# Where the norm products of the next batch stand, and the order of the opening, in an attention and soft-MoE kernel

## The chip, the cores and the metric

One core of a Trainium2 chip runs the whole program. The time is the device time of one execution in microseconds (us), and the median over executions is compared. The profile describes one execution. Its engines are PE (TensorE, matrix products), PEld (its weight loads), DVE (VectorE), ACT (ScalarE), POOL (GpSimd) and SP, whose queue issues every DMA of this kernel.

## The reference, cut to what matters

```python
# 8 batches, 2496 rows, d_qk = 64, d_model = 256
scores = (1 / S) * z @ z.T             # symmetric: queries and keys are both z
out = u * (maximum(scores, 0) ** 2 @ v)
x = out.reshape(19968, 256)
logits = x @ phi                       # 32 slots
slot_input = softmax(logits, axis=0).T @ x
slot_out = relu(slot_input @ w1) @ w2  # 8 experts of 4 slots each
result = softmax(logits, axis=1) @ slot_out
```

The attention is nearly all of the work: for each batch a 2496 x 2496 matrix of scores, its squared positive part, and the product of that with v.

## The kernel before, in words

**Steps.** A batch has five chunks of queries (512 columns, the last one 448) and five blocks of keys (512 rows each). A chunk meets a block in two halves of 256 keys. A chunk therefore has ten halves, a batch fifty (the last batch sixty), and the main loop (L942 to L971) takes one half per step; h counts the steps over all batches, and "place" below means h modulo 50. In a step two things happen. `prepare` (L404) makes ready a half that is needed later: h + 2 in the first 19 steps and h + 3 afterwards. `sums_halves` or `sums_whole` adds the half of this step into `acc`, the product with v.

**Prepare.** If the half is computed, PE multiplies z with z into the PSUM tile `sc`, of which there is one. ACT takes the positive part (`r<-sc`) and squares it (`r<-r`). ACT or DVE casts to fp16 (`ph<-r`), and DVE subtracts to get the rest (`pl<-r,ph`). Because the scores are symmetric, a half that another chunk will need is transposed by DVE (`y<-r`, or `yd<-r` for a part of a diagonal block) and stored in DRAM by a DMA (`turned<-y`). A half that is there already ("turned") is fetched (`r<-turned`), and only the cast and the subtraction are left. At its end `prepare` runs the list `behind`: small work that other parts of the program have put there.

**Sums.** v is held as a high and a low fp16 part, so each half takes twelve products of 512 columns: high and low v with `ph`, high v with `pl`. If the half to be prepared is computed, the sums are cut into two phases of six products, and the product for `sc` and whatever `behind` has for PE stand between the phases.

**The shared bank.** The PSUM pool `ms_ps` holds one tile, and a new tile in it must wait until the last reader of the old one is done. Four users take turns: the norm products (`n<-sq`), the product of `scale_v` (`mx`), the logits of the MoE (`lg<-xg,phi_sb`) and the slot sums (`lg<-xt`, issued together with the logits of the next group of tokens).

**Norms.** z and v of the next batch have to be scaled before they are split into fp16 parts. `load_z` (L124) loads a block of z and gives three actions: `squares` (ACT, tile `sq`, one buffer), `norms` (two products with a matrix of ones into the `ms` tile, a maximum by DVE into `few`, and four small DVE instructions that make the factors `norm2` and `z_by`), and `split` (one ACT and one DVE instruction). The table `splits` (L857 to L868) has the five blocks of batch b loaded at places 19 to 23 of the batch before, squared at 21 to 25, their norms taken at 22 to 26, one step after the squares, and split at 29, 31, 33, 39 and 41. v follows: loads at places 25 to 34, its squares at 27 to 36, `largest` (three small DVE instructions) at 38, `scale_v` (L204: a small product `mx`, a DVE maximum and small DVE instructions) at 40, the splits at 42 to 51.

**Logits.** When two chunks of 512 tokens are complete, `groups` (L251) makes a list of 15 small pieces of MoE work, of which the loop pops one per step at steps with `x.at > 1` (L948). The first piece is the logits with the slot sums of the group before. They fall where the count of pieces puts them: place 22 and 42 for the steps in which the z blocks of batches 1, 2, 4 and 6 are measured, and place 2, 12 and 32 for batches 3, 5 and 7.

**Opening.** L919 to L940: DVE sets a constant, SP issues the loads, PE runs products on a constant (`keep_busy`, tile `idle`) to stay occupied, and for each of the five blocks of z in turn come squares, norms, and the scaling of z in place. After blocks 0 and 1 halves 0 and 1 are prepared. Then come the ten squares of v, `largest`, `scale_v` and the first split, and the loop begins. The first twelve halves are scored from fp32 z.

Of the kernel before, what the change touches and what calls it, by code (L numbers as in the profile page):

```python
# [8 lines left out]
F32 = mybir.dt.float32  # L9
# [9 lines left out]
P = 128  # L19
# [6 lines left out]
QC = 512  # L26
# [35 lines left out]
def bits(ap):  # L62
    return ap.bitcast(I32)
# [14 lines left out]
def attn_soft_moe_kernel(ctx, tc, uT, v, zz, phi, ww, outT):  # L78
# [29 lines left out]
    def pair(name, n):  # L108
        return [cpool.tile([P, n], F32, name=f"{name}{i}") for i in range(2)]

    norm2, z_by, energy, v_by, out_by, few = (
        pair(name, n)
        for name, n in (("norm2", NP), ("z_by", NP), ("energy", 2 * NP), ("v_by", 2 * NP), ("out_by", NP), ("few", 4))
    )

    def take_blocks(b):


        for j in BLOCKS[b == B - 1]:
            zt[b, j] = blk.tile([P, 2, 512], F16, tag="blk", name=f"z_{b}_{j}")  # L120
        for i in range(2 * NP):
            vt_[b, i] = blk.tile([P, 2, 2, D], F16, tag="blk", name=f"v_{b}_{i}")

    def load_z(b, j):  # L124


# [6 lines left out]
        n2, by = (t[b % 2][:, j : j + 1] for t in (norm2, z_by))  # L133
        square = []

        def squares():
            sq = raws.tile([P, 512], BF16, tag="sq", name=f"sq_{b}_{j}", bufs=1)
            act.activation(sq, raw, AF.Square, bias=nudge)
            square.append(sq)

        def norms():
            ps = ms_ps.tile([P, 2, 512], F32, tag="ms", name=f"n2_{b}_{j}")
            for h, rows in enumerate(HALF):
                pe.matmul(
                    ps[:, h, 0:256], ones[rows, 0:P], square[0][rows, 256 * h : 256 * h + 256],
                    start=True, stop=True,
                )
# [22 lines left out]
        return squares, norms, split  # L170

    def load_v(b, i):
        raw = raws.tile([P, 2, D], F32, tag="raw", name=f"vr_{b}_{i}", bufs=NRAW)
        sp.dma_start(raw, v[b, :, 2 * i : 2 * i + 2, :])
        by = v_by[b % 2][:, i : i + 1]

        def squares():
            sq = raws.tile([P, 512], BF16, tag="sq", name=f"vq_{b}_{i}", bufs=1)
# [25 lines left out]
    def scale_v(b):  # L204


        w = few[b % 2]
        ps = ms_ps.tile([P, 2, 512], F32, tag="ms", name=f"mx_{b}")
        for h, rows in enumerate(HALF):
            pe.matmul(  # L210
                ps[:, h, 0:64], w[rows, 0:1].to_broadcast([64, P]), ident[rows, rows],
                start=True, stop=True,
            )
        dve.tensor_reduce(w[:, 2:4], ps[:, :, 0:64], axis=AX.X, op=ALU.max)
        dve.tensor_max(w[:, 1:2], w[:, 2:3], w[:, 3:4])
        dve.tensor_scalar_max(w[:, 1:2], w[:, 1:2], 2.0**-120)
        dve.tensor_scalar(
            bits(w[:, 2:3]), bits(w[:, 1:2]), EXPONENT, EXPONENT, op0=ALU.bitwise_and, op1=ALU.bitwise_xor
        )
        n2 = norm2[b % 2].unsqueeze(2).to_broadcast([P, NP, 2])  # L220
        dve.tensor_scalar(
            v_by[b % 2].rearrange("p (j i) -> p j i", i=2), n2, w[:, 2:3], 2.0**-51, op0=ALU.mult, op1=ALU.mult
        )
        dve.tensor_scalar(
            out_by[b % 2], norm2[b % 2], w[:, 1:2], 2.0**40 / S**2, op0=ALU.mult, op1=ALU.mult
        )
# [350 lines left out]
                work.extend(groups(q))  # L577
            s += w

    late, adding = [], []  # L580


    xt_last = []
# [18 lines left out]
    def groups(q):  # L602
# [17 lines left out]
        def logits():  # L620


            ps = ms_ps.tile([P, 2, 512], F32, tag="ms", name=f"lg_{q}")
            xj = x.rearrange("p c (j t k) -> p c t j k", j=2, k=P)
            for c in range(2):
                for t in range(4):
                    for h, rows in enumerate(HALF):
                        pe.matmul(
                            ps[t * NS : (t + 1) * NS, h, D : 2 * D], phi_sb[rows, c],
                            xj[rows, c, t], start=(c == 0), stop=(c == 1),  # L630
                        )
            if late:
# [224 lines left out]
    splits, later = {}, {}  # L857
    for b in range(1, B):
        base, order = (b - 1) * 2 * NP * NQ, BLOCKS[b == B - 1]
        z_at = [29, 31, 33, 39, 41]  # L860
        v_at = [47, 42, 43, 44, 45, 46, 48, 49, 50, 51]
        for i, (j, at) in enumerate(zip(order, z_at)):
            splits.setdefault(base + 21 + i, []).append((load_z, b, j, [base + 21 + i, base + 22 + i, base + at]))
        for i, at in enumerate(v_at):
            splits.setdefault(base + 27 + i, []).append(
                (load_v, b, i, [base + 27 + i, base + at, base + at])
            )
        later[base + 38] = lambda b=b: largest(b)  # L868
        later[base + 40] = lambda b=b: scale_v(b)
    landing, fetched = {}, set()  # L870

    def transfers(h):

# [13 lines left out]
        for f, b, i, at in splits.get(h + 2, ()):  # L887
            if (b, 0) not in vt_:
                take_blocks(b)
            for step, g in zip(at, f(b, i), strict=True):  # L890
                landing.setdefault(step, []).append(g)
        if h in later:
# [31 lines left out]
    dve.memset(nudge, 2.0**-40)  # L924
    take_blocks(0)
    open_loads()
    constants()
    keep_busy(8)
    for p, (squares, norms) in enumerate(first_z):
        squares()  # L930
        norms()
        if p < 2:
            prepare(p)
        keep_busy(2)
    for f in first_v:
        f()
        keep_busy(2)
    largest(0)
    scale_v(0)
    split_first_v()  # L940
# [1 line left out]
    for h, x in enumerate(halves):  # L942
# [10 lines left out]
        if ahead and not halves[ahead[0]].turned:  # L953
# [318 lines left out]
```

## Time and profile before

| | |
|---|---|
| median of 3 runs | 1422.95 us (1422.49 to 1427.03) |
| the profiled execution's own time | 1428.09 us |
| span of its instructions | 1426.3 us |
| PE busy | 1294.8 us (91%) |
| DVE busy | 1122.3 us (79%) |
| ACT busy | 964.5 us (68%) |
| DMA engines | 69.3% of the span, 210 GB/s |
| granted clock of PE, mean | 0.96 |

A timeline row reads: start, duration, engine, operation, what is written from what, shape, and in brackets how long the engine had been idle and who released it. "x4" products on 64 rows are two pairs that run side by side, one on each half of the array's rows. A product of 512 columns is listed with 0.38 us because its end is modelled; the next one starts 0.216 us later, and that distance is what it costs. A page line of the form "A <- B: 10, 5, 3" in the view of waits means that A waited for B 10 us in total, 5 times, 3 us the longest.

### The profile page before, as it was taken

Reading aid. Unit: us, or ns where it says so; the run is one execution under the profiler, and the core shown is the slowest. Engines: PE = TensorE matmul, PEld = TensorE weight load, DVE = VectorE, ACT = ScalarE, POOL = GpSimd, SP = SyncE. Lnnn points to the kernel's source line nnn. Section 1 sums busy time; section 2 is a strip of 40 time slices with the busy share of each in tenths; the row PEclk is TensorE's granted clock in tenths of the full one; section 3 lists DMA queues with packets and bytes.
Section 4 is the critical chain, followed back from the end, with each engine's and each line's share of the span. In section 5 each row is a group of like instructions: output and inputs, shape, how many; then the busy total and the mean of one; then the engine's idle time right before and its main releaser. Section 6 shows DMA issues by size and latency. Waiting matters only on the chain.

```text
span 1426.3 us, 28005 instructions
## 1 busy us (share of the span) xinstructions
PE 1294.8 (91%) x11069; PEld 618.9 (43%) x11069; DVE 1122.3 (79%) x1685; ACT 964.5 (68%) x1259; POOL 3.7 (0%) x22
## 2 busy tenths in 40 slices
PE   6997999889997999879998999969999899989984
PEld 2343455334543444334553444424454344434752
DVE  4787899588996899768996789857997888867663
ACT  4876788466965878557885768657686668754453
POOL 0000000000000000000000000000000000000000
PEclk9999999999999999989999999989999999999995
DMA  3468838677578747868378855758478874979949
GB/s 126 120 189 246 248 98 213 217 198 225 131 222 259 216 137 179 259 184 254 92 210 260 262 150 140 246 180 232 125 185 256 269 216 115 271 233 298 341 198 383
DMA packets 136404, 298.91 MB, mean 210 GB/s; under 512 B 17872, under 2 KB 38864, under 8 KB 124240
## 3 DMA queue, kind: packets, MB, share of 16 engines
q1 hardware_dynamic: 136272, 297.11, 69.3%
q8 instruction: 87, 1.43, 0.4%
q14 instruction: 45, 0.37, 0.1%
HBM read 162.04 MB, written 113.77 MB: 193 GB/s over the span
## 4 chain that ended last, share of the span: by engine, by line
PE 66%; ACT 14%; DVE 10%; DMA 5%; issue 4%; SPq 1%; DVEq 0%; ACTq 0%
PE acc L74 52%; ACT r L74 8%; PE sc L74 8%; DVE y L74 3%; ACT ph L74 3%; DVE pl L74 3%; PE lg L74 2%; PE pf L74 1%; SPq L74 1%; DMA turned<-y 1%; DMA w_own<-in_w 1%; DVE few L74 1%; DVE ph L74 1%; ACT v L74 1%; ACT ot L74 1%
## 5 line engine op out<-in xcount | busy, mean ns | idle before, releaser
L74 PE MATMUL acc<-ph,v 64*128 64x512 f16 (+5 forms) x5036 | 950.7, 376 | 3.9 <-ACT v L74 2.0
L74 PEld LDWEIGHTS <-v 64*128 64x128 f16 (+1 forms) x7554 | 477.4, 97 | 540.3 <-issue 66.8
L74 PE MATMUL acc<-pl,v 64*128 64x512 f16 (+5 forms) x2518 | 612.0, 376 | 0.3
L74 DVE TENSOR_TENSOR pl<-r,ph 128x1024 f16<-128x1024 f32 (+1 forms) x410 | 466.6, 1145 | 134.5 <-ACT ph L74 108.5
L74 ACT ACTIVATE r<-sc 128x1024 f32<-128x1024 f32 (+1 forms) x242 | 229.3, 947 | 206.9 <-PE sc L74 205.4
L74 ACT CAST ph<-r 128x1024 f16<-128x1024 f32 (+1 forms) x286 | 289.0, 1020 | 118.6 <-PE acc L74 62.6
L74 ACT ACTIVATE r<-r 128x1024 f32<-128x1024 f32 (+1 forms) x242 | 238.8, 987 | 6.9
L74 DVE STREAM_TRANSPOSE y<-r 128x1024 f32<-128x1024 f32 x160 | 198.1, 1238 | 0.0
L74 PE MATMUL sc<-z,z 64*128 64x512 f16 x912 | 124.7, 377 | 2.8 <-ACT r L74 2.5
L74 DVE CAST ph<-r 128x1024 f16<-128x1024 f32 (+1 forms) x124 | 74.2, 599 | 54.3 <-ACT r L74 54.2
L74 PEld LDWEIGHTS <-z 64*128 64x128 f16 x1380 | 71.5, 95 | 78.1 <-issue 10.3
L74 PE MATMUL n<-sq,const-bfloat16-1.0 64*128 64x256 bf16 x80 | 12.9, 316 | 77.6 <-DVE few L74 51.1
L74 DVE SCALAR_TENSOR_TENSOR xg<-acc,out_by,ut 128x1024 f32<-128x1024 f32 (+7 forms) x57 | 51.8, 932 | 20.3 <-PE acc L74 15.9
L74 ACT ACTIVATE v<-vr,v_by 128x512 f16<-128x512 f32 x80 | 57.3, 717 | 2.4 <-DVE v_by L74 2.4
L74 DVE SCALAR_TENSOR_TENSOR v<-vr,v_by,v 128x512 f16<-128x512 f32 x80 | 58.0, 726 | 0.7 <-ACT v L74 0.7
L74 ACT ACTIVATE vq<-vr 128x512 bf16<-128x512 f32 x80 | 49.9, 624 | 10.4 <-DMA vr<-in_v 8.7
L74 PEld LDWEIGHTS <-const-bfloat16-1.0 64*128 64x128 bf16 x156 | 9.3, 112 | 100.8 <-DVE few L74 60.2
L74 PE MATMUL sc<-z 64*128 64x512 f16 (+1 forms) x468 | 51.2, 324 | 0.0
L74 DVE STREAM_TRANSPOSE y<-xg 128x512 f32<-128x512 f32 x72 | 49.5, 687 | 0.0
L74 DVE TENSOR_TENSOR pl<-rd,ph 128x512 f16<-128x512 f32 x36 | 24.2, 672 | 23.6 <-ACT ph L74 23.6
L74 DVE COPY ot<-pf 128x1024 f32<-128x1024 f32 (+1 forms) x20 | 24.0, 1198 | 20.6 <-PE pf L74 19.8
L74 ACT ACTIVATE sq<-zr,nudge 128x512 bf16<-128x512 f32 x35 | 25.1, 718 | 21.4 <-PE n L74 18.6
(177 smaller groups left out, 620.4 us busy)
## 6 DMA issues: line engine op xcount, KB each, us to landing
turned<-y SPq DMA_DIRECT2D x320, 256.0 KB, 4.5
r<-turned SPq DMA_DIRECT2D x76, 1024.0 KB, 6.3
xt<-y SPq DMA_DIRECT2D x288, 72.0 KB, 3.2
vr<-in_v SPq DMA_DIRECT2D x80, 256.0 KB, 5.3
outT<-ot SPq DMA_DIRECT2D x18, 1024.0 KB, 6.9
ut<-in_uT SPq DMA_DIRECT2D x31, 512.0 KB, 5.9
lent<-yd SPq DMA_DIRECT2D x144, 64.0 KB, 2.0
rd<-lent SPq DMA_DIRECT2D x36, 256.0 KB, 5.3
```

Source lines behind the costliest of these rows:

```text
L74: return lambda *a, **k: self.tc.keep_in_program_order(f(*a, **k))
```

## The change

- **Later norms.** The five blocks of z are loaded at places 9, 11, 13, 15 and 17. A new function, `measure`, runs in every step. It takes a block's norm products only if its squares were issued at least two steps before, if neither norms nor logits have used the bank in this step or the one before, and, up to place 25, only if the half being prepared is computed. It then issues the squares of the next block if fewer than two squared blocks are waiting. `sq` has two buffers, and the squares of v have a tile of their own.
- **Small steps once per batch.** The DVE maximum goes into `tops`; the four small instructions move into `factors`, which runs once for all five blocks. `scale_v` uses one instruction in place of two.
- **Places.** The splits of z move from 29, 31, 33, 39, 41 to 31, 32, 33, 39, 41, and `scale_v` from 40 to 41.
- **Opening.** An ACT instruction on the constant is issued ahead of the first data. The five squares follow one another, and the norm products go to five different PSUM places, so that none waits for another's maximum. z blocks are scaled one by one as they are needed. Halves 0 to 3 are prepared ahead of the loop, with the squares of v between them; steps 0 and 1 of the loop prepare nothing.

```diff
         def squares():
-            sq = raws.tile([P, 512], BF16, tag="sq", name=f"sq_{b}_{j}", bufs=1)
+            sq = raws.tile([P, 512], BF16, tag="sq", name=f"sq_{b}_{j}", bufs=2)
...
-        def norms():
-            ps = ms_ps.tile([P, 2, 512], F32, tag="ms", name=f"n2_{b}_{j}")
+        def norms(ps=None):
+            if ps is None:
+                ps = ms_ps.tile([P, 2, 512], F32, tag="ms", name=f"n2_{b}_{j}")[:, :, 0:256]
...
-            w = few[b % 2][:, 0:2]
-            dve.tensor_reduce(w, ps[:, :, 0:256], axis=AX.X, op=ALU.max)
-            dve.tensor_max(n2, w[:, 0:1], w[:, 1:2])
-            dve.tensor_scalar(bits(n2), bits(n2), EVEN, None, op0=ALU.bitwise_and)
-            dve.tensor_scalar(
-                bits(by), bits(n2), EVEN, 1, op0=ALU.bitwise_xor, op1=ALU.logical_shift_right
-            )
-            dve.tensor_scalar_mul(by, by, 2.0**77)
-            if b == 0:
-                dve.tensor_scalar_mul(raw, raw, by)
+            dve.tensor_reduce(tops[b % 2][:, 2 * j : 2 * j + 2], ps, axis=AX.X, op=ALU.max)
...
+    def factors(b, js=slice(0, NP)):
+        n2, by = (t[b % 2][:, js] for t in (norm2, z_by))
+        t = tops[b % 2].rearrange("p (j h) -> p h j", h=2)[:, :, js]
+        dve.tensor_max(n2, t[:, 0], t[:, 1])
...
-        z_at = [29, 31, 33, 39, 41]
+        z_at = [31, 32, 33, 39, 41]
...
-            splits.setdefault(base + 21 + i, []).append((load_z, b, j, [base + 21 + i, base + 22 + i, base + at]))
+            splits.setdefault(base + 11 + 2 * i, []).append((load_z, b, j, base + at))
...
-        later[base + 40] = lambda b=b: scale_v(b)
+        later[base + 41] = lambda b=b: scale_v(b)
...
+    unmeasured, squared, used = [], [], [-9, 0]
+
+    def measure(h, scoring):
+        n = h % (2 * NP * NQ)
+        if squared and squared[0][0] <= h - 2 and used[0] <= h - 2 and (scoring or n >= 26):
+            behind.append(squared.pop(0)[1])
+            used[0] = h
+            used[1] += 1
+            if used[1] % NP == 0:
+                behind.append(lambda: factors(used[1] // NP))
+        if unmeasured and unmeasured[0][0] <= h and len(squared) < 2:
+            _, squares, norms = unmeasured.pop(0)
+            behind.append(squares)
+            squared.append((h, norms))
...
+    act.activation(few[1][:, 0:1], nudge, AF.Square)
     constants()
+    keep_busy(6)
...
+    for p in range(NP):
+        first_z[p][0]()
+    first_z[0][1](places[0])
+    factors(0, slice(0, 1))
+    raise_z(0)
+    for p in range(1, NP):
+        keep_busy(1)
+        first_z[p][1](places[p])
+    factors(0, slice(1, NP))
+    raise_z(1)
+    for p in range(4):
+        measure_v((2, 2, 1, 1)[p])
+        prepare(p)
+        if p < 3:
+            raise_z(p + 2)
     keep_busy(8)
...
+    measure_v(4)
     largest(0)
     scale_v(0)
     split_first_v()
...
         if work and (x.at > 1 or last <= 20):
+            n = len(bursts)
             work.pop(0)()
+            if len(bursts) > n:
+                used[0] = h
         behind.extend(landing.pop(h, ()))
-        ahead = [k for k in range(h + 2 + (h > CATCH), h + 3 + (h >= CATCH)) if k < len(halves)]
+        ahead = [k for k in range(h + 2 + (h > CATCH), h + 3 + (h >= CATCH)) if k < len(halves) and k >= 4]
+        measure(h, ahead and not halves[ahead[0]].turned)
...
+        if not ahead and h < 2:
+            run(middle)
+            run(turning)
+            run(behind)
+            sums_halves(h, acc, 1, sums_halves(h, acc, 0, None))
```

More of the change, by code (lines that the diff above doesn't have):

```diff
@@ L109, in pair @@
         return [cpool.tile([P, n], F32, name=f"{name}{i}") for i in range(2)]
-    norm2, z_by, energy, v_by, out_by, few = (
+    tops, norm2, z_by, energy, v_by, out_by, few = (
         pair(name, n)
-        for name, n in (("norm2", NP), ("z_by", NP), ("energy", 2 * NP), ("v_by", 2 * NP), ("out_by", NP), ("few", 4))
+        for name, n in (("tops", 2 * NP), ("norm2", NP), ("z_by", NP), ("energy", 2 * NP), ("v_by", 2 * NP), ("out_by", NP), ("few", 4))
     )
@@ L132, in load_z @@
         zraw[b, j] = raw
-        n2, by = (t[b % 2][:, j : j + 1] for t in (norm2, z_by))
+        by = z_by[b % 2][:, j : j + 1]
         square = []
         def squares():
-            sq = raws.tile([P, 512], BF16, tag="sq", name=f"sq_{b}_{j}", bufs=1)
+            sq = raws.tile([P, 512], BF16, tag="sq", name=f"sq_{b}_{j}", bufs=2)
             act.activation(sq, raw, AF.Square, bias=nudge)
             square.append(sq)
-        def norms():
-            ps = ms_ps.tile([P, 2, 512], F32, tag="ms", name=f"n2_{b}_{j}")
+        def norms(ps=None):
+            if ps is None:
+                ps = ms_ps.tile([P, 2, 512], F32, tag="ms", name=f"n2_{b}_{j}")[:, :, 0:256]
             for h, rows in enumerate(HALF):
                 pe.matmul(
-                    ps[:, h, 0:256], ones[rows, 0:P], square[0][rows, 256 * h : 256 * h + 256],
+                    ps[:, h], ones[rows, 0:P], square[0][rows, 256 * h : 256 * h + 256],
                     start=True, stop=True,
                 )
-            w = few[b % 2][:, 0:2]
-            dve.tensor_reduce(w, ps[:, :, 0:256], axis=AX.X, op=ALU.max)
-            dve.tensor_max(n2, w[:, 0:1], w[:, 1:2])
-            dve.tensor_scalar(bits(n2), bits(n2), EVEN, None, op0=ALU.bitwise_and)
-            dve.tensor_scalar(
-                bits(by), bits(n2), EVEN, 1, op0=ALU.bitwise_xor, op1=ALU.logical_shift_right
-            )
-            dve.tensor_scalar_mul(by, by, 2.0**77)
-            if b == 0:
-                dve.tensor_scalar_mul(raw, raw, by)
+            dve.tensor_reduce(tops[b % 2][:, 2 * j : 2 * j + 2], ps, axis=AX.X, op=ALU.max)
         def split():
@@ L170, in load_z @@
         return squares, norms, split
+    def factors(b, js=slice(0, NP)):
+        n2, by = (t[b % 2][:, js] for t in (norm2, z_by))
+        t = tops[b % 2].rearrange("p (j h) -> p h j", h=2)[:, :, js]
+        dve.tensor_max(n2, t[:, 0], t[:, 1])
+        dve.tensor_scalar(bits(n2), bits(n2), EVEN, None, op0=ALU.bitwise_and)
+        dve.tensor_scalar(
+            bits(by), bits(n2), EVEN, 1, op0=ALU.bitwise_xor, op1=ALU.logical_shift_right
+        )
+        dve.tensor_scalar_mul(by, by, 2.0**77)
     def load_v(b, i):
@@ L177, in squares @@
         def squares():
-            sq = raws.tile([P, 512], BF16, tag="sq", name=f"vq_{b}_{i}", bufs=1)
+            sq = raws.tile([P, 512], BF16, tag="vq", name=f"vq_{b}_{i}", bufs=1)
             act.activation(
@@ L214, in scale_v @@
         dve.tensor_reduce(w[:, 2:4], ps[:, :, 0:64], axis=AX.X, op=ALU.max)
-        dve.tensor_max(w[:, 1:2], w[:, 2:3], w[:, 3:4])
-        dve.tensor_scalar_max(w[:, 1:2], w[:, 1:2], 2.0**-120)
+        dve.scalar_tensor_tensor(w[:, 1:2], w[:, 2:3], 2.0**-120, w[:, 3:4], op0=ALU.max, op1=ALU.max)
         dve.tensor_scalar(
@@ L578, in finish_chunk @@
             s += w
-    late, adding = [], []
+    late, adding, bursts = [], [], []
     xt_last = []
@@ L631, in logits @@
                         )
+            bursts.append(q)
             if late:
@@ L889, in transfers @@
                 take_blocks(b)
+            if f is load_z:
+                *two, split = f(b, i)
+                unmeasured.append((h + 2, *two))
+                landing.setdefault(at, []).append(split)
+                continue
             for step, g in zip(at, f(b, i), strict=True):
@@ L926, in attn_soft_moe_kernel, with raise_z, measure_v @@
     open_loads()
+    act.activation(few[1][:, 0:1], nudge, AF.Square)
     constants()
-    keep_busy(8)
[L929 to L937, printed above, removed]
+    keep_busy(6)
+    places = [ms_ps.tile([P, 2, 512], F32, tag="ms", name="n2_first")]
+    places.append(acc_ps.tile([P, 2, QC], F32, tag="acc", name="n2_second"))
+    places = [t[:, :, 256 * i : 256 * i + 256] for t in places for i in range(2)] + [idle[:, :, 0:256]]
+    def raise_z(p):
+        dve.tensor_scalar_mul(zraw[0, p], zraw[0, p], z_by[0][:, p : p + 1])
+    def measure_v(n):
+        for _ in range(n):
+            first_v.pop(0)()
+    for p in range(NP):
[13 more added lines that the diff above has]
+            raise_z(p + 2)
+    keep_busy(8)
+    measure_v(4)
     largest(0)
@@ L948, in attn_soft_moe_kernel @@
         if work and (x.at > 1 or last <= 20):
+            n = len(bursts)
             work.pop(0)()
+            if len(bursts) > n:
+                used[0] = h
         behind.extend(landing.pop(h, ()))
-        ahead = [k for k in range(h + 2 + (h > CATCH), h + 3 + (h >= CATCH)) if k < len(halves)]
+        ahead = [k for k in range(h + 2 + (h > CATCH), h + 3 + (h >= CATCH)) if k < len(halves) and k >= 4]
+        measure(h, ahead and not halves[ahead[0]].turned)
         split_first_v()
-        if ahead and not halves[ahead[0]].turned:
+        if not ahead and h < 2:
[3 more added lines that the diff above has]
+            sums_halves(h, acc, 1, sums_halves(h, acc, 0, None))
+        elif ahead and not halves[ahead[0]].turned:
             turn = sums_halves(h, acc, 0, None)
```

## The prediction, made before the changed kernel ran

> **What bounds the kernel now.** I read the page first, then the view of waits, then the timeline around the largest waits. The page says that PE is the engine to look at:
>
> ```profile
> span 1426.3 us, 28005 instructions
> PE 1294.8 (91%) x11069; PEld 618.9 (43%) x11069; DVE 1122.3 (79%) x1685; ACT 964.5 (68%) x1259; POOL 3.7 (0%) x22
> ```
>
> PE is listed as busy for 91% of the span, so shorter work on another engine is worth only what it takes out of the other 131.5 us (1426.3 - 1294.8) or out of PE's own pace. The view of waits says where much of that idle time is (who waited <- for whom: us in total, times, longest):
>
> ```profile
> PE n L74 <- DVE few L74: 51.1, 19, 4.2
> PE n L74 <- DVE slot_acc L74: 19.8, 3, 6.6
> PE mx L74 <- DVE few L74: 14.2, 8, 2.0
> PE n L74 <- DVE L L74: 1.4, 1, 1.4
> ACT ph L74 <- DMA r<-turned: 48.9, 14, 5.6
> ```
>
> The norm products, which are nothing in themselves, stop PE for 51.1 + 19.8 + 1.4 = 72.3 us, and `mx` for 14.2. The last row is ACT waiting for fetches; it matters further down. The timeline of batch 2's blocks, steps 71 to 76, shows why the norm products wait:
>
> ```profile
> 263.55 0.81 PE L74 MATMUL sc<-z 64*128 64x512 f16 x6
> 264.40 1.02 ACT L74 ACTIVATE r<-sc 128x1024 f32<-128x1024 f32 x1 [1.93 <-PE sc L74]
> 265.46 1.06 ACT L74 ACTIVATE r<-r 128x1024 f32<-128x1024 f32 x1
> 265.59 1.09 PE L74 MATMUL lg<-xg,phi_sb 64*32 64x256 f32 x32
> ...
> 266.47 1.07 PE L74 MATMUL lg<-xt 64*32 64x256 f32 x32
> 266.55 0.69 DVE L74 CAST ph<-r 128x1024 f16<-128x1024 f32 x1 [2.63 <-ACT r L74]
> ...
> 268.50 0.70 DVE L74 STREAM_TRANSPOSE yd<-r 128x512 f32<-128x512 f32 x1
> ...
> 275.64 0.41 DVE L74 TENSOR_TENSOR slot_acc<-slot_acc,lg 128x256 f32<-128x256 f32 x1
> 276.20 0.40 PE L74 MATMUL n<-sq,const-bfloat16-1.0 64*128 64x256 bf16 x2 [6.61 <-DVE slot_acc L74]
> 276.37 1.09 PE L74 MATMUL acc<-ph,v 64*128 64x512 f16 x4
> ...
> 281.49 0.92 PE L74 MATMUL sc<-z,z 64*128 64x512 f16 x6
> ...
> 282.35 0.61 PE L74 MATMUL acc<-ph,v 64*128 64x512 f16 x4
> ...
> 284.94 0.82 PE L74 MATMUL sc<-z,z 64*128 64x512 f16 x6
> ```
>
> PE issues in program order, and a norm product that finds the bank occupied holds up every product behind it. At 276.20 it had waited 6.61 us for the last reader of the slot sums that were issued at 266.47. That reader stands in DVE's queue behind everything that `prepare` gave DVE in the same step, and ACT works on that first.
>
> The stop costs twice. The twelve products of the step at 276.37 take until 281.49, 5.12 us; those of the step at 282.35 take until 284.94, 2.59 us. After a long wait PE runs at half pace for a while. The window of this stretch shows it as a granted clock of 0.88 (columns: window, length, busy time of PE, PEld, DVE, ACT, POOL, clock, DMA share, GB/s):
>
> ```profile
> 262.20:304.00 41.80, 28.25 (x273) 12.55 (x274) 25.36 (x50) 19.21 (x25) 0.00 (x0) 0.88 0.56 169
> ```
>
> **Part 1, the norm products.** Of the 72.3 us, two waits of 0.7 us lie in the opening, which leaves 70.9 us in the seven later batches. How long the bank stays occupied is read from a pair of rows of batch 3, product and maximum:
>
> ```profile
> 436.64 0.27 PE L74 MATMUL n<-sq,const-bfloat16-1.0 64*128 64x256 bf16 x2
> 443.61 0.69 DVE L74 TENSOR_REDUCE few<-n 128x2 f32<-128x512 f32 x1
> ```
>
> From the product to the end of its maximum: 443.61 + 0.69 - 436.64 = 7.7 us, one of the longest, since other MoE work stands ahead of the maximum there. In step 71 the same chain can be added up: `sc` starts at 263.55 and the sums go on 0.65 us later, so a norm product behind it would be issued at 264.2; its maximum would follow the transpose that ends at 268.50 + 0.70 = 269.2, and take 0.69: 269.9, so 5.7 us. The slot sums held the bank from 266.47 to 276.05, 9.6 us.
>
> A step with scores takes PE 2.59 us of sums and 0.65 of scores, 3.24 us; two are 6.5 us. Following the conditions of `measure` place by place puts the norm products at 13, 15, 17, 21, 24 for batch 1; 13, 21, 24, 26, 28 for batches 2, 4, 6; 14, 21, 23, 25, 27 for batches 3, 5, 7. Seventeen of them follow another by two steps. For fourteen that is 6.5 us against 5.7 to 7.7, so each waits nothing to 1.2 us; I take 0.4, 6 us in all (0 to 17). Behind the logits at 22 the product at 24 comes after the slot sums (1.0), a step (3.24), another step (3.24) and half the sums with scores (1.95), 9.4 us against 9.6: nothing. The other three are those at 28 in batches 2, 4 and 6: the step has no scores and its products stand first, so the distance is 1.3 + 3.24 = 4.5 us against 5.7: 1.2 us, three times, 4 us.
>
> But `measure` looks only backwards. In batches 1, 2, 4 and 6 a norm product stands at 21 and the logits at 22, and nothing holds the logits back. The price follows from the sum just made: the bank is free at 269.9, the logits are due at 265.59, so they wait 4.3 us, and a slow stretch of 1.4 us follows (the lower end of those of part 2). Four times 5.7 is 23 us. It is bounded below by nothing (if the logits did not need the whole tile) and above by 6.6 + 2.5 us, the worst row of before, four times: 36.
>
> **Part 2, the slow stretches.** There are twelve in these batches, each behind a wait of 3 us or more, the first from 276.37, the last this one:
>
> ```profile
> 1108.51 1.06 PE L74 MATMUL acc<-ph,v 64*128 64x512 f16 x4
> ...
> 1112.39 0.81 PE L74 MATMUL sc<-z,z 64*128 64x512 f16 x6
> ```
>
> Twelve products in 3.88 us instead of 2.59: 1.3 us lost, against 2.5 in the first. Measured the same way the twelve come to 1.1 to 2.5 each, 20 us in all. Not every wait of 3 us has one, but without such waits they go.
>
> Here a row and the Trainium skill differ:
>
> ```profile
> 288.84 0.39 PE L74 MATMUL n<-sq,const-bfloat16-1.0 64*128 64x256 bf16 x2 [3.08 <-DVE few L74]
> 289.03 1.06 PE L74 MATMUL acc<-ph,v 64*128 64x512 f16 x4
> ```
>
> A wait of 3.08 us was enough: the four products that follow carry 1.06, as those at half pace do (1.09 at 276.37), not 0.61. The Trainium skill, "TensorE: Matmul & The Clock Gate", section "Part 1: The HAM clock gate", says that PE's clock is halved after an idle window of about 3.4 us. By that rule the five stretches behind waits of about 3.1 us would not be there, and the gain of this part would be some 7 us less; no term here uses it.
>
> **Part 3, `mx`.**
>
> ```profile
> 172.31 0.44 PE L74 MATMUL mx<-ident,few 64*128 64x64 f32 x4 [1.60 <-DVE few L74]
> 172.69 0.55 PE L74 MATMUL acc<-ph,v 128*128 128x448 f16 x2
> ...
> 174.97 0.54 PE L74 MATMUL acc<-ph,v 128*128 128x448 f16 x2
> ...
> 176.30 0.29 DVE L74 TENSOR_REDUCE few<-mx 128x2 f32<-128x128 f32 x1
> ...
> 177.33 1.09 PE L74 MATMUL lg<-xg,phi_sb 64*32 64x256 f32 x32
> ```
>
> Of 14.2 us, 1.9 lie in the opening; 12.3 remain, 1.6 to 2 per batch, because `largest` is late on DVE. At 41 the product stands one step of 2.28 us later (174.97 - 172.69), and this wait goes. In batches 1, 2, 4 and 6 the logits stand at 42. In before two steps lay between; now there is one, and the bank is held from 172.31 to 176.59, 4.28 us, of which `mx` and one step cover 0.4 + 2.28. That leaves 1.6 us, four times: 6 (0 to 16, the 16 if the step were no cover at all: 4 x 3.9).
>
> **Part 4, small DVE steps.** Four instructions per block run once per batch instead of five times; this row is one of them (busy, mean ns, idle before):
>
> ```profile
> L74 DVE TENSOR_TENSOR norm<-few 128x1 f32<-128x1 f32 x40 | 6.4, 160 | 1.4
> ```
>
> They are on DVE, which does not set the pace here, so I cost them at nothing; were DVE the bound, 16 x 0.16 x 7 = 18 us would be won.
>
> **Part 5, the opening.**
>
> ```profile
> 3.63 1.28 ACT L74 ACT_TABLE_LOAD   x1 [3.63 <-DMA cw<-in_zz]
> 4.93 0.72 ACT L74 ACTIVATE sq<-cw,nudge 128x512 bf16<-128x512 f32 x1
> ...
> 29.25 0.63 ACT L74 ACTIVATE vq<-vr 128x512 bf16<-128x512 f32 x1
> ...
> 30.01 0.17 DVE L74 TENSOR_SCALAR v_by<-energy 128x10 int32<-128x10 int32 x1 [4.83 <-ACT vq L74]
> ...
> 33.14 0.61 PE L74 MATMUL acc<-ph,v 64*128 64x512 f16 x2 [1.97 <-ACT v L74]
> ...
> 43.28 0.59 PE L74 MATMUL acc<-ph,v 64*128 64x512 f16 x4
> ```
>
> ACT is now the chain. From 3.63, when the first z is there and the table load is already done, it has five squares of 0.72 (3.6 us), ten squares of v at a distance of 30.01 - 29.25 = 0.76 (7.6), four halves of two passes (1.02 and 1.06 in the rows of step 71; 8.3), and one cast that I put at 1: 20.5 us, and I add 2 us (0 to 4) in which it waits for the first scores. That ends at 26.2; before, `largest` started at 30.01. The sums, 3.13 us behind it, start at 29.3. Before, step 2 began at 43.28, 10.1 us behind the first sums, because two fp32 score products and the slow pace lay in between. Now steps 0 and 1 have 24 products: one step cold (5.1), one warm (2.6), 7.7 us, and 0.5 for v's splits. Step 2 begins at 37.5: 5.8 us won. With ACT later and both steps cold it is 2, with all warm 9. I take 5.
>
> **What moves beside.** The loads of z stand ten steps earlier in SP's queue, in front of the fetches for chunk 2. The three splits at 31, 32, 33 stand one step before the loads of v that reuse their buffers, so SP waits there as it already does for the third. Cover: a half is prepared three steps early, so a fetch may be late by some 5 us before PE sees it. But the DMA engines have little room in that stretch:
>
> ```profile
> 246.00:254.00 8.00, 8.00 (x42) 3.51 (x38) 6.39 (x8) 3.43 (x6) 0.00 (x0) 1.00 0.96 305
> ```
>
> I take 3 us for all this (0 to 35; the second rival explains the 35).
>
> **The sum.** Removed: 70.9 + 20 + 12.3 = 103. To this come 5 us: the view counts a wait from the listed end of the last product, and a pair of products is listed with 0.61 (at 282.35) where the next could start after 0.43, so each of some thirty waits is 0.18 us longer than listed; 108. Left or new: 23 + 6 + 4 + 6 + 3 = 42 (the logits after a norm product, the fourteen, the three, the logits after `mx`, the transfers). Won: 66, and 5 in the opening, 71 us. On the profiled execution: 1428.09 - 71 = 1357. That execution lies 5.1 us above the median of the runs; its waits follow from the order of the program and should be the same in the others, so the median goes from 1422.95 to **1352 us**, for this case 1334 to 1370.
>
> **Rivals.** *The logits do not wait.* Then 23 us more are won: 1329. For it: the norm products use columns 0 to 255 and the logits the other half. Against: the row "PE n <- DVE L" is a norm product waiting for a reader of the logits' columns alone.
>
> *The lead is used up by fetches.* ACT waits 48.9 us for fetches, now all behind the three steps' lead. With PE faster by 5% and z's loads in front, part comes through. If 70% do, 34 us: 1386. For: a DMA share of 0.96 over eight us. Against: in that very stretch PE is busy throughout.
>
> *DVE falls behind (slower).* If DVE has more work per step than PE at places 13 to 28, PE runs ahead until the lead of three steps is used, and a maximum ends 9.7 us behind its product. The seventeen products two steps behind another, and the four behind the logits, wait 9.7 - 6.5 = 3.2 us (67) with a slow stretch of 1.4 each (29), the logits 9.7 - 1.3 = 8.4 and 1.4 each (39), and 6 stay at `mx`: 141 against the 108 removed, minus 5 in the opening: 1423 + 28 = 1451. It decides from the point where DVE's work there exceeds PE's. The window at 262.20 has 25.36 us of DVE; of PE's 41.8 us, 13.6 are idle (28.25 busy) and 4 are slow pace, which leaves 24 of work; and with this change one of its five maxima (0.69) and 16 of its 20 small instructions (2.6) leave it. 22 against 24: it should not happen, but the margin is only a tenth.
>
> *It does not do what it says.* If the tile framework still ties each product to something one step back, all stays but the opening: 1418 to 1423.
>
> **Chances.** Forecast 0.59, no wait of the logits 0.14, fetches 0.19, DVE behind 0.05, nothing 0.03. A measurement of this kernel can tell about 0.3%, 4.3 us, from no change. Faster 0.93, same 0.03, slower 0.04 (part of the DVE case would only eat the gain). The range, 1322 to 1390, takes in the first three cases with their bounds.
>
> **What would show it.** In the changed profile: "PE n <- DVE few" under 10 us and "PE n <- DVE slot_acc" nearly gone; a new row "PE lg <- DVE few" (or the weight loads of `lg`) of about 4.3 us four times and 1.6 four times; rows of 1.06 for `acc` only behind those and in the opening; first sums near 29 us, step 2 near 37.5. Wrong it is if PE's waits turn up at `acc` or `sc` instead, on ACT or on DMA, or if PE's idle time falls and the span does not.

## The result, and the profile after

| | before | after |
|---|---|---|
| median | 1424.05 us (1422.49 to 1427.03, 4 runs) | 1376.89 us (1375.57 to 1379.91, 4 runs) |
| ratio | | 0.967, 95% interval 0.9645 to 0.9694 |
| the profiled execution's own time | 1428.09 us | 1376.17 us |
| its span | 1426.3 us | 1374.0 us |
| granted clock of PE, mean | 0.96 | 0.977 |

The kernel is faster by 47 us by the medians and by 52 us by the profiled executions. The forecast was 71 us. The page after:

```profile
span 1374.0 us, 27763 instructions
PE 1275.1 (93%) x11029; PEld 618.3 (45%) x11029; DVE 1102.6 (80%) x1553; ACT 960.5 (70%) x1260; POOL 3.7 (0%) x22
```

PE's idle time is down from 131.5 us to 98.9 (1374.0 - 1275.1), and its busy time by 19.7 us (1294.8 - 1275.1). Only 40 of 11069 products are fewer, so nearly all of that is pace, not work. DVE has lost 20 us and ACT 4. The view of waits after:

```profile
ACT ph L74 <- DMA r<-turned: 49.9, 15, 5.3
ACT vq L74 <- DMA vr<-in_v: 49.8, 20, 6.6
...
ACT sq L74 <- DMA zr<-in_zz: 24.8, 9, 4.0
...
PE lg L74 <- DVE tops L74: 16.9, 4, 4.7
...
PE sc L74 <- ACT r L74: 13.9, 22, 1.7
...
PE lg L74 <- DVE few L74: 12.1, 4, 3.3
...
PE n L74 <- DVE tops L74: 8.8, 9, 1.8
...
PE mx L74 <- DVE few L74: 3.6, 2, 3.2
...
PE n L74 <- DVE slot_acc L74: 3.0, 3, 1.0
```

The norm products' 72.3 us have become 8.8 + 3.0, and `mx` has 3.6 left of 14.2. The two rows of `lg` are the logits that now wait instead, four times each: for the maximum of a norm product (`tops`) and for that of `mx` (`few`). Three rows were small before: ACT's wait for the loads of z ahead of their squares (2.8 us, now 24.8), its wait for the loads of v (now 49.8), and PE's wait at `sc` for ACT (now 13.9). The last two, before:

```profile
ACT vq L74 <- DMA vr<-in_v: 8.7, 9, 2.5
...
PE sc L74 <- ACT r L74: 2.5, 8, 0.6
```

The timeline after, at the place that the prediction worked out for step 71:

```profile
261.82 0.81 PE L74 MATMUL sc<-z 64*128 64x512 f16 x6
...
262.46 0.27 PE L74 MATMUL n<-sq,const-bfloat16-1.0 64*128 64x256 bf16 x2
...
267.41 0.70 DVE L74 STREAM_TRANSPOSE yd<-r 128x512 f32<-128x512 f32 x1
268.04 0.65 DVE L74 TENSOR_REDUCE tops<-n 128x2 f32<-128x512 f32 x1
...
268.75 1.96 PE L74 MATMUL lg<-xg,phi_sb 64*32 64x256 f32 x32 [4.72 <-DVE tops L74]
...
270.46 1.90 PE L74 MATMUL lg<-xt 64*32 64x256 f32 x32
...
272.29 0.60 PE L74 MATMUL acc<-ph,v 64*128 64x512 f16 x4
```

The norm product is issued at once, 0.64 us behind the scores. Its maximum stands behind the transpose, as in the sum, and the logits of the next step wait 4.72 us for it. Then the 64 products of the logits and slot sums take 3.54 us (272.29 - 268.75), because PE runs at half pace behind the wait (the granted clock of this stretch is 0.52); without a wait they take 1.89. The same thing behind `mx` in batch 1:

```profile
167.20 0.44 PE L74 MATMUL mx<-ident,few 64*128 64x64 f32 x4 [0.42 <-DVE few L74]
...
168.25 1.22 DVE L74 TENSOR_TENSOR pl<-r,ph 128x1024 f16<-128x1024 f32 x1
...
169.39 0.74 DVE L74 SCALAR_TENSOR_TENSOR z<-zr,z_by,z 128x512 f16<-128x512 f32 x1
...
170.05 2.35 DVE L74 TENSOR_TENSOR pl<-r,ph 128x1024 f16<-128x1024 f32 x2
...
172.32 0.74 DVE L74 SCALAR_TENSOR_TENSOR z<-zr,z_by,z 128x512 f16<-128x512 f32 x1
...
172.98 0.28 DVE L74 TENSOR_REDUCE few<-mx 128x2 f32<-128x128 f32 x1
...
173.32 1.96 PE L74 MATMUL lg<-xg,phi_sb 64*32 64x256 f32 x32 [3.30 <-DVE few L74]
```

`mx` is done at 167.64, but its maximum starts only at 172.98: in DVE's queue three subtractions and two parts of z's splits stand ahead of it, without a gap between them. The logits wait 3.30 us. The opening after:

```profile
0.73 1.28 ACT L74 ACT_TABLE_LOAD   x1 [0.73 <-PEq L1316]
...
25.99 0.17 DVE L74 TENSOR_SCALAR v_by<-energy 128x10 int32<-128x10 int32 x1 [0.89 <-ACT vq L74]
...
29.19 0.61 PE L74 MATMUL acc<-ph,v 64*128 64x512 f16 x2 [1.78 <-ACT v L74]
...
36.98 0.59 PE L74 MATMUL acc<-ph,v 64*128 64x512 f16 x4
```

`largest` starts at 25.99 (26.2 foretold), the first sums at 29.19 (29.3), step 2 at 36.98 (37.5). Against 43.28 before that is 6.3 us won.

To see where the rest comes from I took the start of each step's sums in both traces and subtracted. Chunks 2 and 3 (places 20 to 39) of the first seven batches won 67.4 us. Chunk 4 (places 40 to 49) lost 14.6, of which 16.4 at the places where batches 1, 2, 4 and 6 are scaled and the logits follow `mx`, and 1.8 came back in the others. All the rest together lost 6.8. With the opening: 67.4 + 6.3 - 14.6 - 6.8 = 52.3, the difference of the spans.

### The profile page after: what moved, and what is told of

It reads as the page before. It is cut to its first block, busy times and chain, and to the rows that moved or that the text cites. A ratio compares the mean times of both kernels' runs of the same rounds, so it can differ in the third digit from the quotient of the medians.

```text
span 1374.0 us, 27763 instructions
## 1 busy us (share of the span) xinstructions
PE 1275.1 (93%) x11029; PEld 618.3 (45%) x11029; DVE 1102.6 (80%) x1553; ACT 960.5 (70%) x1260; POOL 3.7 (0%) x22
## 4 chain that ended last, share of the span: by engine, by line
PE 46%; ACT 17%; DVE 13%; DMA 11%; SPq 7%; issue 5%; DVEq 0%; ACTq 0%; POOLq 0%
PE acc L74 35%; ACT r L74 9%; SPq L74 7%; PE sc L74 5%; DMA turned<-y 5%; ACT ph L74 4%; DVE pl L74 4%; DVE y L74 4%; PE lg L74 2%; DMA vr<-in_v 2%; PE pf L74 1%; ACT vq L74 1%; DMA w_own<-in_w 1%; DVE ph L74 1%; DMA zr<-in_zz 1%
## 5 line engine op out<-in xcount | busy, mean ns | idle before, releaser
L74 PE MATMUL acc<-ph,v 64*128 64x512 f16 (+5 forms) x5036 | 934.9, 370 | 4.2 <-ACT v L74 1.8
L74 PE MATMUL acc<-pl,v 64*128 64x512 f16 (+5 forms) x2518 | 604.1, 369 | 2.7 <-DVE pl L74 2.1
L74 ACT CAST ph<-r 128x1024 f16<-128x1024 f32 (+1 forms) x286 | 287.5, 1017 | 87.6 <-DMA r<-turned 49.9
L74 ACT ACTIVATE vq<-vr 128x512 bf16<-128x512 f32 x80 | 49.8, 623 | 50.3 <-DMA vr<-in_v 49.8
L74 ACT ACTIVATE v<-vr,v_by 128x512 f16<-128x512 f32 x80 | 56.9, 715 | 11.8 <-DVE v_by L74 11.8
L74 DVE SCALAR_TENSOR_TENSOR xg<-acc,out_by,ut 128x1024 f32<-128x1024 f32 (+7 forms) x57 | 51.8, 931 | 13.3 <-PE acc L74 13.2
L74 PE MATMUL lg<-xg,phi_sb 64*32 64x256 f32 x608 | 25.5, 443 | 29.0 <-DVE tops L74 16.9
L74 ACT ACTIVATE sq<-zr,nudge 128x512 bf16<-128x512 f32 x35 | 25.0, 714 | 24.8 <-DMA zr<-in_zz 24.8
L74 ACT COPY ot<-pf 128x1024 f32<-128x1024 f32 (+1 forms) x20 | 19.8, 991 | 24.3 <-PE pf L74 18.1
```

Of the source, the lines that this page charges most:

```text
L74: return lambda *a, **k: self.tc.keep_in_program_order(f(*a, **k))
```

## The experiments

**Theories.** A: what is left of the waits is logits that follow another user of the bank by one step, at 22 behind a norm product and at 42 behind `mx`. B (the rival for the missing gain): PE is held up through ACT, which stands at the squares of v until their loads have landed. All diffs are against the kernel after, and all ratios against the kernel before on the same chip. The experiments ran on three chips, where the kernel before had medians of 1422.5 to 1425.86 us; so a difference of some 3 us between the medians of two experiments says nothing. Starts of steps are compared as above, between the profiled executions.

**1. Hold the norm product when the logits are next.**

```diff
+        soon = work and work[0].__name__ == "logits" and halves[h + 1].at > 1
-        if squared and squared[0][0] <= h - 2 and used[0] <= h - 2 and (scoring or n >= 26):
+        if squared and squared[0][0] <= h - 2 and used[0] <= h - 2 and (scoring or n >= 26) and not soon:
```

> The changed kernel (1376.9 us), but a norm product is held back when the logits are the next step's piece, so those at place 21 of batches 1, 2, 4, 6 move to 24. Theory A (what is left is logits that follow another user of the bank by one step): the waits of the logits for a maximum of z (PE lg <- DVE tops, 16.9 us) and the half pace of those four bursts (4 x 1.6) vanish: some 20 us less, 1357. Theory B (PE has run out of prepared halves there, because ACT and DVE are late; the logits only show it): the same time reappears as waits of acc and sc, 1371 to 1377.

1358.98 us, ratio 0.9535 (0.9504 to 0.9565): 17.9 us less than the kernel after. The row of `lg` waiting for `tops` is gone; the one for `few` remains:

```profile
PE lg L74 <- DVE few L74: 11.2, 4, 2.8
...
PE n L74 <- DVE tops L74: 9.4, 10, 1.8
```

The norm product that was held goes elsewhere without a wait: its own row hardly grows (8.8 to 9.4). For place 22, A is right.

**2. `mx` back at 40.**

```diff
-        later[base + 41] = lambda b=b: scale_v(b)
+        later[base + 40] = lambda b=b: scale_v(b)
```

> The changed kernel, but the product of scale_v back at place 40. Theory A: the four waits of the logits for few (12.1 us) and their half pace (4 x 1.6) go, and seven waits of mx of 1.6 to 2.1 us (13) come back: 5 us less, 1372. Had the move to 41 been worth what the prediction gave it (12.3 - 6), it would be 6 us more, 1383.

1385.91 us, ratio 0.9704 (0.9667 to 0.974), 9 us more than the kernel after, where A expected 5 less: a miss. It is near the other value named, 1383, which is what the prediction's own sum gave the move. The intervals overlap (0.9667 and 0.9694), but in the profiled execution, the slowest of the four (1389.95), the starts of the steps show the loss where `mx` stands: places 30 to 39, with the wait of `mx` behind them, take 19.9 us more, places 40 to 49 take 10.7 less. The logits lose their wait for `few`, but `mx` gets a larger one than it had in the kernel before (14.2):

```profile
PE mx L74 <- DVE few L74: 18.0, 8, 3.4
```

In batch 1 it is 2.34 us there, 1.60 before. It fits that PE comes to place 40 earlier while `largest` stands as deep in DVE's queue as ever, but that was not tried. The waits alone nearly cancel: 14.4 us more for `mx` (18.0 - 3.6), 12.1 less for the logits. Pace is the larger part: in batches 1, 3, 5 and 7 the granted clock is 0.59 to 0.70 over the 4 us that begin with `mx`, which had waited 2.22 to 2.66 us; in batches 2 and 4, behind 1.58 us, it is 1.00. The move to 41 is worth its price, by these places.

**3. `largest` at 37 and `mx` at 40.** The same distance of three places as in the change, but both a step earlier, so that two steps lie between `mx` and the logits.

```diff
-        later[base + 38] = lambda b=b: largest(b)
-        later[base + 41] = lambda b=b: scale_v(b)
+        later[base + 37] = lambda b=b: largest(b)
+        later[base + 40] = lambda b=b: scale_v(b)
```

> The changed kernel, with largest at place 37 and the product of scale_v at 40: three steps between them and two to the logits. Theory A: neither mx nor the logits at 42 wait; 12.1 + 6.4 us less, 1358. Theory B (the maximum of mx is late because a fetch is late, whatever the distance): the logits still wait most of it, 1368 to 1377.

1373.49 us, ratio 0.9639 (0.9607 to 0.967), 3.4 us less, an interval that overlaps that of the kernel after.

```profile
PE mx L74 <- DVE few L74: 6.9, 5, 3.2
...
PE lg L74 <- DVE few L74: 3.3, 4, 0.9
```

The logits' wait falls from 12.1 to 3.3 as A has it, and `mx` takes back 3.3 (6.9 - 3.6). The waits alone would give 5.5 us. The run gave less than A expected (1358) and lies where the rival put it (1368 to 1377), but not for the rival's reason: the logits do not keep most of their wait. The starts of the steps say where the rest is: places 40 to 49 take 15.4 us less than in the kernel after, places 30 to 39 take 8.9 more. Of these, 3.3 are the wait of `mx` and about 2.6 its own products (7 x 0.37), which now count there; the other 3 stay open. The maximum of `mx`, in batch 2:

```profile
326.45 0.44 PE L74 MATMUL mx<-ident,few 64*128 64x64 f32 x4
...
332.06 0.28 DVE L74 TENSOR_REDUCE few<-mx 128x2 f32<-128x128 f32 x1
```

It ends 5.9 us behind the product (332.06 + 0.28 - 326.45), although `mx` stands at 40 again, where in the kernel before it was 4.3 to 4.4. The section after the experiments comes back to this.

**4. The splits of z back at 29, 31, 33.** For B: are these splits what delays the loads of v into their buffers?

```diff
-        z_at = [31, 32, 33, 39, 41]
+        z_at = [29, 31, 33, 39, 41]
```

> The changed kernel, with the splits of z back at 29, 31, 33. Theory B (the splits at 31, 32, 33 free the buffers for the last loads of v one step later, ACT waits for v's squares and PE then at sc): ACT vq <- DMA vr falls from 49.8 us to about 10, the waits at sc by 5 to 10 us, the time to 1368 to 1372. Theory A: nothing changes, 1377, even if the waits of vq fall.

1377.97 us, ratio 0.9668 (0.9638 to 0.9698): no difference. ACT's wait for the loads of v is still 41.9 us of 49.8. The places of the splits are not what makes it large.

**5. The new opening alone.** The schedule of before, with the opening of after and `sq` in two buffers. The shorter `scale_v` and the tile for v's squares stay too.

```diff
+            if b:
+                factors(b, slice(j, j + 1))
...
-        z_at = [31, 32, 33, 39, 41]
+        z_at = [29, 31, 33, 39, 41]
...
-            splits.setdefault(base + 11 + 2 * i, []).append((load_z, b, j, base + at))
+            splits.setdefault(base + 21 + i, []).append((load_z, b, j, [base + 21 + i, base + 22 + i, base + at]))
...
-        later[base + 41] = lambda b=b: scale_v(b)
+        later[base + 40] = lambda b=b: scale_v(b)
...
-            if f is load_z:
-                *two, split = f(b, i)
-                unmeasured.append((h + 2, *two))
-                landing.setdefault(at, []).append(split)
-                continue
```

> The kernel before with the new opening alone (the five squares need two buffers, so z's squares have two throughout): loads, norm products, small steps and splits of the later batches at the places of before. The step starts of the changed kernel put the opening's share at 6 us (step 2 at 36.98 instead of 43.28); if it is independent of the rest: 1418. If the earlier start is given back where the first transposed halves come back from DRAM: 1424.

1415.97 us, ratio 0.9958 (0.9935 to 0.998), which is 6.5 us less than before. The norm products wait as before:

```profile
PE n L74 <- DVE tops L74: 48.8, 18, 4.2
...
PE n L74 <- DVE slot_acc L74: 19.8, 3, 6.6
```

So the opening's share stands by itself, and the other 39 us (1415.97 - 1376.89) are the schedule's.

**6. One step between users of the bank instead of two.**

```diff
-        if squared and squared[0][0] <= h - 2 and used[0] <= h - 2 and (scoring or n >= 26):
+        if squared and squared[0][0] <= h - 2 and used[0] <= h - 1 and (scoring or n >= 26):
```

> The changed kernel, but a norm product may stand one step behind another user of the bank instead of two; the squares stay two steps ahead. The products of a batch then stand at places like 21, 23, 24, 25. Theory A (the bank is held 5.7 to 7.7 us, so one step of 3.2 is too short): waits of 1.5 to 4 us come back for two or three products per batch and behind the logits, some with a slow stretch: 25 to 35 us more, 1402 to 1412. Rival (what helped was to take squares and loads away from the logits and maxima, not the distance): 1375 to 1382.

1420.91 us, ratio 0.9974 (0.9948 to 1.0001), 44 us more than the kernel after. More was lost than A expected (25 to 35). The profiled execution, the fastest of the ten (1411.68):

```profile
PE n L74 <- DVE tops L74: 24.0, 12, 3.5
...
PE n L74 <- DVE slot_acc L74: 20.4, 6, 3.5
```

The two rows are 44.4 us where the kernel after has 11.8, and stretches of `acc` at half pace, summed as in the prediction's second part, are back at 13.3 us (3.8 after, 22.2 before). The norm products still stand two steps behind their squares here, the small steps still run once per batch, and the opening is the new one. Without the distance on the bank the gain outside the opening is gone. Whether the distance would bring it alone, without the earlier loads and squares, was not tried. By the starts of the steps, places 10 to 29 take 44.5 us more than in the kernel after, and places 30 to 39 take 11.4 less; ACT's wait for the loads of v, which stand at the same places, falls there from 49.8 to 29.2.

**7. Experiment 1, and the logits put off by a step behind `mx`.**

```diff
...
+        scaled.add(base + 41)
...
-        if work and (x.at > 1 or last <= 20):
+        after_mx = work and work[0].__name__ == "logits" and h - 1 in scaled
+        if work and (x.at > 1 or last <= 20) and not after_mx:
```

> The run with the norm product held back before the logits (1359.0 us), and the logits too wait a step more when the product of scale_v stood in the step before (place 43 instead of 42 in batches 1, 2, 4, 6). Theory A: 11.2 us of waits of the logits for few and 4 x 1.6 us of half pace go, with one us per batch left: 1345. Rival (the maximum of mx is late because a fetched half is late, 3.8 us in batch 1; one step more gives back only what a step covers, and the stall moves to acc): 1354 to 1359.

1349.44 us, ratio 0.9488 (0.9448 to 0.9528), 9.5 us less than experiment 1 and midway between A's 1345 and the rival's 1354. The wait is down from 11.2 to 2.3, and another one appears inside the logits, for the turned tokens of the slot sums:

```profile
PE lg L74 <- DMA xt<-y: 8.6, 6, 3.7
...
PE lg L74 <- DVE few L74: 2.3, 4, 0.6
```

The waits go as A has it for place 42 too, and no stall moves to `acc`, as the rival had it: both kinds of logits together are worth 27.5 us.

**8. The first seven loads of v two steps earlier, against the schedule of after.**

```diff
-            splits.setdefault(base + 27 + i, []).append(
+            splits.setdefault(base + 27 + i - 2 * (i < 7), []).append(
```

> The changed kernel, with the first seven loads of v two steps earlier; the squares stay where they are. Theory B (ACT stands at v's squares for loads, 49.8 us in all against 8.7 before, and PE then waits at sc): the waits of vq fall below 20 us, those of sc (13.9 us, some 4 of them in the opening) by 5 or more, 1368 to 1372. Rival: ACT has room there, nothing changes, 1377.

1365.92 us, ratio 0.9604 (0.9574 to 0.9633), 11 us less than the kernel after. The profiled execution is the slowest of the six runs (1371.05); its waits show the link that B claims:

```profile
PE sc L74 <- ACT r L74: 6.2, 11, 1.3
...
ACT vq L74 <- DMA vr<-in_v: 1.2, 3, 0.6
```

ACT's wait for the loads has gone from 49.8 to 1.2 us, and PE's wait for ACT at `sc` from 13.9 to 6.2. B is right, beside A and not in its place. Of the 48.6 us that ACT no longer waits, PE saw 11: most of the lateness was covered by the lead of the prepared halves. By the starts of the steps the gain is at places 30 to 39, 11.9 us. The profiled execution keeps only 4.8 us of it in its span (1374.0 - 1369.2); 3.3 of the rest are logits at place 42 that ran at half pace behind waits of 2.81 and 2.82 us, behind which the kernel after ran at full pace (the last section has more of this).

**9. The four small instructions for each block again.**

```diff
             dve.tensor_reduce(tops[b % 2][:, 2 * j : 2 * j + 2], ps, axis=AX.X, op=ALU.max)
+            if b:
+                factors(b, slice(j, j + 1))
...
-            if used[1] % NP == 0:
-                behind.append(lambda: factors(used[1] // NP))
```

> The changed kernel, but the four small instructions run behind each block's maximum again, five times per batch instead of once: 16 more DVE instructions of 0.16 us per batch, 18 us of DVE in all. Theory (DVE does not set the pace): within 0.3% of 1376.9. Rival (DVE is close enough to the bound): up to 18 us more, 1385 to 1395.

1384.84 us, ratio 0.972 (0.9689 to 0.975), 8 us more by the medians and 5.6 by the profiled spans (1379.6 - 1374.0). That is outside the 0.3% of the theory (1381.0) and at the edge of the rival's range (1385 to 1395). The intervals just overlap (0.9694 and 0.9689), so the size is uncertain; that it is nothing is unlikely but not excluded.

```profile
PE n L74 <- DVE tops L74: 10.4, 9, 2.3
```

That row explains 1.6 us (10.4 - 8.8). PE is listed as busy for 3.5 us longer (1278.6) with the same number of products, which is pace; one such place is named in the last section. So this run doesn't show that the instructions themselves cost the 8 us.

**10. Experiments 7 and 8 together.** The diffs are those of 1, 7 and 8.

> The norm product held back before the logits, the logits put off behind the product of scale_v (these two: 1349.4 us), and the first seven loads of v two steps earlier (alone 11 us less than the changed kernel). If the three causes are separate, their gains add: 1338 to 1341. If ACT's lateness at v's squares and the stops at the logits are two sides of one thing (a stop of PE gives the loads time), less than half of the 11 remains: 1344 to 1349.

1339.78 us (1338.97 to 1343.9), ratio 0.9412 (0.9381 to 0.9442): the best version. Added singly, 27.5 and 11.0 give 38.5; together they are 37.1.

```profile
PE sc L74 <- ACT r L74: 7.0, 11, 2.2
...
PE lg L74 <- DVE few L74: 2.3, 4, 0.8
...
ACT vq L74 <- DMA vr<-in_v: 0.9, 3, 0.4
```

The causes of A and B are separate, and each is removed at its own place.

**11. Without the early ACT instruction.**

```diff
     open_loads()
-    act.activation(few[1][:, 0:1], nudge, AF.Square)
     constants()
```

> The changed kernel without the ACT instruction on the constant ahead of the first data. Theory (ACT is the chain of the opening): the table load of 1.28 us falls behind the first block again and the first sums start 1.3 us later, at 30.5 instead of 29.19. Rival (PE or the loads set the opening's pace): unchanged, 29.2.

One execution, 1378.64 us. Its opening:

```profile
3.56 1.28 ACT L74 ACT_TABLE_LOAD   x1 [3.56 <-DMA cw<-in_zz]
...
30.37 0.61 PE L74 MATMUL acc<-ph,v 64*128 64x512 f16 x2 [1.78 <-ACT v L74]
...
38.72 0.60 PE L74 MATMUL acc<-ph,v 64*128 64x512 f16 x4
```

The table load falls behind the first data again, and the first sums stand 1.18 us later (30.37 - 29.19), step 2 by 1.74 (38.72 - 36.98). At step 2, 1.74 of the opening's 6.3 us hang on this one instruction.

## Why the prediction was right in direction and too large

The mechanism was the one forecast; the sum was too large through sizes. Its terms, against the profiled execution after:

| term | predicted, us | measured, us |
|---|---|---|
| waits of norm products, less what is left of them | 70.9 - 10 = 60.9 | 70.9 - 11.8 = 59.1 |
| slow stretches of `acc` | 20 | 18.4 (22.2 to 3.8) |
| waits of `mx` outside the opening | 12.3 | 11.9 (0.4 left) |
| logits at 22 | -23 | -22.3 (16.9 of waits, 5.4 of half pace) |
| logits at 42 | -6 | -13.7 (12.1 and 1.6) |
| transfers | -3 | about -11 (experiment 8) |
| opening | 5 | 6.3 |
| listing of waits | 5 | not measured |

- **Norm products, slow stretches, opening: right.** Experiment 6 shows that the two steps on the bank are needed for it, experiment 5 that the opening adds its own. The early table load was counted rightly as well (experiment 11). The size of the slow stretches depends on the smallest that is counted: with 0.25 us as the least, and all batches outside the opening, they are 24.9 us before, 2.0 after and 12.6 in experiment 6. The prediction put twelve of them behind waits of 3 us or more; two more stand behind waits of `mx` of only 1.97 us (last section).
- **Logits at 22: right in place, number and size.** The half pace was expected in the `acc` products behind; it fell on the logits themselves.
- **Logits at 42: mis-sized by 8.** The step that failed is "the bank is held from 172.31 to 176.59, 4.28 us, of which `mx` and one step cover 0.4 + 2.28. That leaves 1.6 us". The holding time was carried over from a product that had itself just waited 1.60 us for DVE, the wait that the change takes away. DVE's queue does not become shorter by that: at 41 the bank is held 173.26 - 167.20 = 6.1 us in batch 1 (172.98 + 0.28 is the maximum's end), so the logits wait 3.3. It is not the place that does it, for in experiment 3, at 40, it is 5.8 to 5.9 us. Counted from PE's arrival at `mx`, its wait included, the maximum ends 5.9 to 6.3 us later in the seven batches before and 5.6 to 6.5 after. With 1.60 + 4.28 = 5.9 in place of 4.28 the prediction's own sum gives 3.2 us. Experiment 7 removes the wait for 9.5 us.
- **Transfers: mis-sized by 8.** "I take 3 us for all this" looked at the fetches for the halves, and these were indeed covered: that row is 49.9 after and 48.9 before. What came late were the loads of v. They stand at the same places, in the stretch that became shorter by 67 us over the batches: the lead in steps is the same, in microseconds it is not. That more lead removes the wait is shown (experiment 8), and that z's splits don't cause most of it (experiment 4); that the shorter stretch is the cause fits experiment 6, where the stretch is longer again and the wait smaller (29.2), but what the earlier loads of z add wasn't tried by itself. ACT's new wait for those loads (24.8 us) is as large in the best version (23.4); what it costs isn't known. The rival "the lead is used up by fetches" had the mechanism, with the wrong load and three times the price.
- **From the profiled execution to the median: 5 us.** "Its waits follow from the order of the program and should be the same in the others" failed. The profiled execution of before lies 4.0 us above its median (1428.09 and 1424.05), that of after 0.7 below. The excess belonged to that execution. What differs between executions stays open.
- **Small steps: not nothing.** Experiment 9 puts them at some 5 to 8 us, with the doubt named there; the prediction had them at nothing because DVE does not set the pace. The measured column adds up to about 49 without the listing and 54 with it, against 52.3, and the other count of the slow stretches would add some 4. So the account closes to within about 6 us, and where the small steps' gain lies among the terms isn't shown.
- **The other rivals.** The logits do wait, so the whole bank is shared. DVE did not become the bound: 80% busy, and the row of norm products waiting for it is 8.8 us. And the change did what it says.
- **The clock rule.** The Trainium skill, "TensorE: Matmul & The Clock Gate", section "Part 1: The HAM clock gate", asks for an idle window of about 3.4 us before the clock is halved. Behind waits listed with 4.7 us the pace was halved, in agreement; waits of 1.97 us in the kernel before and of 2.82 us in experiment 9 (both below) had half pace behind them too, which that figure doesn't cover.

## What to carry to other kernels

When several users take turns on one PSUM tile, look in both directions: a rule that keeps a user two steps behind the last one must also keep the next user away from it, and here the forward half was worth 27.5 us more. The time for which a tile is held is not a property of its user but of the queue in which its last reader stands. Count it from the moment at which the user arrives, with its own wait included: a wait that is taken away there can come back as holding time, as 1.6 us did here. And a load issued so many program steps ahead loses lead in microseconds whenever the steps in front of it get faster; after a gain, look at the rows of loads that were small.

## What the hardware showed that I had not expected

Equal waits are not followed by equal pace. In the kernel before, `mx` waited 1.97 us in batch 3 and in batch 5, and the same products follow (below each row the window that begins with it; its last three columns are the granted clock, the DMA share and GB/s):

```profile
501.73 0.44 PE L74 MATMUL mx<-ident,few 64*128 64x64 f32 x4 [1.97 <-DVE few L74]
```

```profile
501.73:506.10 4.37, 4.37 (x26) 2.38 (x27) 4.33 (x6) 1.67 (x2) 0.00 (x0) 1.00 0.76 273
```

```profile
833.07 0.44 PE L74 MATMUL mx<-ident,few 64*128 64x64 f32 x4 [1.97 <-DVE few L74]
```

```profile
833.07:837.50 4.43, 4.43 (x18) 2.06 (x19) 4.39 (x6) 0.86 (x1) 0.00 (x0) 0.68 0.74 261
```

The granted clock is 1.00 in the one and 0.68 in the other, and eighteen products of `acc` that take 3.41 us in the one (505.51 - 502.10) take 5.10 in the other (838.54 - 833.44). The same holds for longer waits: the logits behind `mx` waited 2.81 us in the kernel after (at 334.84) and ran at full pace, the 64 products in 1.89 us at a clock of 1.00; in experiment 9 they waited 2.82 us (at 966.60) and took 3.16 us at a clock of 0.58. And behind two waits of 3.85 us in the kernel before (300.74 and 631.73) the next 4 us have a clock of 1.00, behind a third of the same length (963.02) 0.67. So between about 2 and 3.9 us half pace comes by chance or by something that these traces don't show. It makes the price of a wait uncertain by more than a microsecond, and it may be a part of why executions of one kernel differ (experiment 6 ran from 1411.68 to 1427.09); that was not tested.
